# Reordering the loads ahead of the first expert layer: the second batch's rows before weight block 5, and the rows for the last transform in column halves

## The chip, the cores and the metric

The kernel runs on one core of one Trainium2 chip. The metric is the device time of one execution in microseconds; the median of several runs is what is compared.

## The reference

Two stages, joined by a reshape. First a spectral mixing of each of 8 sequences of 3008 rows and 256 channels: a real Fourier transform along the rows, a product with a complex filter, and the inverse transform. Then a two-layer perceptron with the activation h / (1 + exp(-h)) on all 24064 rows.

```python
X = np.fft.rfft(x, axis=1)                      # x: (8, 3008, 256)
Y = X * (filt_r + 1j * filt_i)[None]
y = np.fft.irfft(Y, n=3008, axis=1)
t = y.reshape(24064, 256)
h = t @ w_in                                    # w_in: (256, 2048)
g = h * (1.0 / (1.0 + np.exp(-h)))
out = g @ w_out                                 # w_out: (2048, 256), float64 on entry like w_in
```

## The kernel before, in words

**The steady part.** The transforms are written as small matrix products (3008 = 47 x 64). The perceptron goes in 48 pairs of token groups by 8 steps; each step does a hidden part (`hidden`, matmuls of L756 into px and pyz) and a projection (`project`, L819 into acc), with a scheme that trades matmuls for sums. While one batch is in the perceptron, the transforms of the next one are worked in between the steps, at places listed by hand (`plan`, `put`). The order of the instructions on every engine is that of the program text.

**The opening.** Nothing can be hidden for the first batch (batch 0), so its transforms stand ahead of the first step. In order:

- Weight blocks 0 to 3 and the rows of batch 0 are loaded; small matmuls (`idle`) run meanwhile. Each weight block j is two loads of 256 KB, `raw`, one of w_in (L926) and one of w_out (L929). The weights come as 64-bit floats and are turned into 32-bit ones by hand: `bits` (DVE), `converted` (ACT), `rounded` and `placed` (DVE).
- ACT, SP and POOL load the filters and the tables (`load_filters`, d_t, e_t). SP then loads the table of the last transform into `wi_t` and weight blocks 4 to 7.
- `stage1_first`, `forward`, `multiply`, `add`, `inverse_first`: the first transform, the second, the filter and the inverse of the second, in 6 groups g. `rows_first` (L541, L543) copies each group's result out of PSUM into two tiles q and stores each to `d2` in DRAM, 256 KB a store: ten stores from ACT's queue, two from SP's.
- `second["load_two"]` loads the first two of batch 1's eight pieces (768 KB) into `x_all` on SP, and weight block 8 is queued behind it. `stage1_first` reads x_all before that, as part of batch 0's rows.
- The rows of d2 (48 of them, for two halves h) come back into `t4`, for groups 0 to 3 of `stage3`, the last transform. `load_t4_rows(k)` (L571) loads the 16 rows that groups 2k and 2k + 1 of the inverse have made: one load for each h, 16 packets of 16 KB. `SPREAD` says on which partitions the 16 rows stand, and the table in wi_t has its rows in the same places (`ws_tbl`). Six loads in all, on SP.
- While they come, DVE and ACT convert weight blocks 4 to 8, PE runs the first transform of batch 1's two pieces (`stage1`, L345), and then 16 filler products (`idle_wide`, L1055), which write a bank that nobody reads.
- `stage3(0)` to `stage3(3)` (L586) run on PE; `copy` (L600) evicts them to `y` on ACT and DVE. When PE has read wi_t for the last of them, SP reloads it in the plain order (L1173), then loads batch 1's third and fourth pieces and weight blocks 10 to 13.
- From y, `tokens` makes the sums ty, and the first step begins (px, L756).

The loads and stores of SP's and ACT's queues carry completion semaphores that are used again in turn.

Of the kernel before, what the change touches and what calls it, by code (L numbers as in the profile page):

```python
# [56 lines left out]
NS, NG = 24, 6  # L57
# [12 lines left out]

SPREAD = (32, 1), (1, 2), (0, 2)


ORDER = [i for g in range(NG) for i in (g, g + 6, 17 - g, 23 - g)]
# [94 lines left out]
def kernel(  # L171
# [9 lines left out]
    nc = tc.nc  # L181
    ctx.enter_context(tc.manual_schedule())

    wf_host, wx_host, wq_host, wi_host, d_host, e_host = dft_tables()
# [1 line left out]
    wx_dram = nc.inline_tensor(wx_host, name="wx_tbl")  # L186
    wq_dram = nc.inline_tensor(wq_host, name="wq_tbl")
    wi_dram = nc.inline_tensor(wi_host, name="wi_tbl")
    ws_host = wi_host.copy()
    for k, (first, by) in enumerate(SPREAD):  # L190
        for h in range(2):
            ws_host[64 * h + first:64 * h + first + 15 * by + 1:by] = wi_host[64 * h + 16 * k:64 * h + 16 * k + 16]
    ws_dram = nc.inline_tensor(ws_host, name="ws_tbl")
    d_dram = nc.inline_tensor(d_host, name="d_tbl")
    e_dram = nc.inline_tensor(e_host, name="e_tbl")

# [26 lines left out]
    wi_t = cpool.tile([128, N1], FP32)  # L223
# [27 lines left out]
    def bank(b, name, spare=None):  # L251


        if early[0] is None and spare in ("x", "yz"):
            return xps.tile([128, 2, C], FP32, name=name, tag=spare)
        if early[0] is None and spare is not None:
            return accps.tile([128, 2, C], FP32, name=name, tag=f"a{spare}")
        if early[0] is None:
            return fps.tile([128, 2, C], FP32, name=name, tag="f")
        early[0] += 1  # L260
        k = early[0] % 8
        if k < 2:
            return fps.tile([128, 2, C], FP32, name=name, tag="f")
        if k > 5:
            return xps.tile([128, 2, C], FP32, name=name, tag="x" if k == 6 else "yz")
        return accps.tile([128, 2, C], FP32, name=name, tag=f"a{k - 2}")

    def spectral(b):
# [3 lines left out]
        d2 = dpool.tile([2 * NS, 32, 2, C] if b > 0 else [2 * NS, 2, 32, C], FP32, name=f"d2_{b}", tag="d2")  # L272
        xs, us, t2s, banks, prods, halves, t4s = {}, {}, {}, {}, {}, {}, {}
# [290 lines left out]
                rows = d2[:, h, 4 * g:4 * g + 4] if b == 0 else d2[:, 4 * g:4 * g + 4, h, :]  # L564
                nc.sync.dma_start(out=t4s[g][64 * h:64 * h + 2 * NS], in_=rows)

        def load_t4_rows(k, queue=None):

            first, by = SPREAD[k]
            for h in range(2):  # L570
                (queue or nc.sync).dma_start(out=us["t4"][64 * h + first:64 * h + first + 15 * by + 1:by],  # L571
                                  in_=d2[16 * k:16 * k + 16, h, 0:16])

        def stage3(g, home=None):

# [26 lines left out]
        def evict_y(g, h):  # L602
# [4 lines left out]

        return dict(us=us, store_rows=store_rows, evict_y=evict_y, evict_t1=evict_t1, halves=halves, load_first=load_first, stage1_first=stage1_first, fill_first=fill_first, load_x=load_x, load_two=load_two, sums=sums, stage1=stage1, reverse_x=reverse_x,
                    load_fold=load_fold, fold=fold, stage1_fold=stage1_fold, evict_fold=evict_fold,
                    load_t2=load_t2, forward=forward, multiply=multiply, add=add, inverse=inverse, inverse_first=inverse_first, rows_first=rows_first, even=even, rows=rows, load_t4=load_t4, load_t4_rows=load_t4_rows, stage3=stage3)  # L610

    pending = []

# [290 lines left out]
    def load_weights(j, queue=None):  # L904

        if j in (8, 11, 12, 13):
            pool, tag = (t4pool, "t4") if j in (11, 12) else (upool, "u")
            raw = pool.tile([128, 2, 512], U32, name=f"raw_{j}", tag=tag)
        else:

            if j in (0, 2):
                t = ypool.tile([128, 2, HALF], FP32, name=f"raw_{j}", tag="y")
                raws.setdefault("tiles", []).append(t)
                raws["at"] = t.rearrange("p a n -> p (a n)").bitcast(U32)[:, 0:2048]
                raws["y"] = raws["at"]
                raws.setdefault("first", raws["at"])
            elif j == 4:
                raws["at"] = spool.tile([128, 2048], U32, name=f"raw_{j}", tag="s")
            elif j == 6:
                raws["at"] = gpool.tile([128, 2048], U32, name=f"raw_{j}", tag="g")  # L920
            elif j in (9, 14):
                raws["at"] = raws["y"]
            at = 1024 * (j in (1, 3, 5, 7, 10, 15))
            raw = raws["at"][:, at:at + 1024].rearrange("p (w n) -> p w n", w=2)
        queue = queue or nc.sync
        queue.dma_start(  # L926
            out=raw[:, 0].rearrange("p (a n) -> p a n", a=2),
            in_=moe_w_in.bitcast(U32)[:, 256 * j:256 * j + 256].rearrange("(a p) n -> p a n", p=128))
        queue.dma_start(out=raw[:, 1], in_=moe_w_out.bitcast(U32)[128 * j:128 * j + 128, :])  # L929
        raws[j] = raw  # L930
# [78 lines left out]
    def weights(*js, queue=None):  # L1009
        for j in js:  # L1010
            if wide:
                load_weights(j, queue)
# [5 lines left out]
    def converted(*js):  # L1018
        if wide:
            convert_weights(*js)  # L1020
# [30 lines left out]
    def idle_wide(n, ps=None, rhs=None):  # L1051

        ps = ps or bank(0, "idle")
        for _ in range(n):
            nc.tensor.matmul(out=ps[:, 0], lhsT=wx_t, rhs=wide_rows if rhs is None else rhs,  # L1055
                             start=True, stop=True)

    wide_rows = d_t[0:96].rearrange("p s r n -> p (s r n)")[:, 0:256]
    idle(27)

    part, second = spectral(0), spectral(1)
    weights(0, 1, 2, 3)
    place = part["load_first"]()
# [10 lines left out]
    load_filters(queues, 4, 2 * NG)  # L1074
    nc.scalar.dma_start(out=d_t[:, 16:NS], in_=d_dram[:, 16:NS])
    nc.scalar.dma_start(out=e_t[:, 2:NG], in_=e_dram[:, 2:NG])
    nc.sync.dma_start(out=wi_t, in_=ws_dram.ap())
    weights(4, 5, 6, 7)

    signed = []  # L1080
    for i in range(2):
        t = typool.tile([128, 2, 2, 2, 128], FP32, name=f"signed_{i}", tag="ty")
# [26 lines left out]
    for k in range(16):  # L1109
        part["stage1_first"](k, 2)  # L1110
        if k in whole:
            part["stage1_first"](whole[k], 3)
    second["load_two"]()
    weights(8)
    part["forward"](0, fill=4)
    placed(0, 1)
    for g in range(1, 4):
# [31 lines left out]
    inverse(5)  # L1149
    bits(6, 7, 8)  # L1150
    for k in range(2):
        part["load_t4_rows"](k)
    part["load_t4_rows"](2)
    converted(4, 5)
    placed(2, 3)
    weights(9)
# [10 lines left out]
    gp.tensor_copy(out=gate, in_=w_t[:, 4, A11, 0, 0:1])  # L1167
    for u in range(2):
        second["store_rows"](u)
    idle_wide(16)  # L1170
    for g in range(4):
        part["stage3"](g)
    nc.sync.dma_start(out=wi_t, in_=wi_dram.ap())  # L1173
    second["load_x"](2)
    weights(10, 11, 12)
    second["load_x"](3)
# [7 lines left out]
    for b in range(1, B):  # L1184
        plan(b, second if b == 1 else spectral(b))
# [81 lines left out]
```

## Time and profile before

| | |
|---|---|
| median of 3 runs | 2579.2 us (2575.68 to 2580.06) |
| the profiled execution | 2579.25 us, of which its span is 2577.4 us |
| mean granted clock of TensorE | 0.995 |
| PE, DVE, ACT, POOL busy | 99%, 65%, 42%, 17% of the span |
| first stage 3 matmul that runs on, first px | 69.10 us, 76.94 us |

The profile is of one execution. Times in it are microseconds from the start of the span. PE is the matmul, PEld the load of its stationary operand, DVE, ACT, POOL and SP are the vector, scalar, GpSimd and sync engines; a q behind an engine's name is its sequencer, which issues DMAs. The matmuls of 32-bit floats stand in the profile as two records each. "x_all<-in_x_dram" is a transfer from the input x to the tile x_all.

### The profile page before, as it was taken

To read this page: it belongs to the slowest core of one execution; us is meant where nothing else is said; L and a number is where in the kernel's file an instruction comes from. 1 tells how busy PE (TensorE), PEld (TensorE's weight loads), DVE (VectorE), ACT (ScalarE), POOL (GpSimd) and SP (SyncE) were. 2 spreads that over 40 slices of the span, in tenths; PEclk is the share of its full clock that TensorE was granted. 3 is DMA by queue.
4 is the path that set the end of the run, shared out by engine and by line. 5 is a ranking of instruction groups with operands and counts; after the bars stand their busy time and mean duration, and the time that the engine had idled before them with its cause. 6 is when DMAs were issued, how large, how long until landed. Compare 5 with 4: busy or idle time off the path is not lost.

```text
span 2577.4 us, 47850 instructions
## 1 busy us (share of the span) xinstructions
PE 2553.1 (99%) x18714; PEld 2196.6 (85%) x18714; DVE 1664.4 (65%) x3589; ACT 1090.4 (42%) x3019; POOL 430.3 (17%) x688
## 2 busy tenths in 40 slices
PE   8999999999999999999999999999999999999998
PEld 6688888888888888888888888888888888888987
DVE  7766666676666666666666676666666666555554
ACT  3544444444444444444444444444444444444443
POOL 4212111111122111311121111211121112101101
PEclk9899999999999999999999999999999999999999
DMA  9522232222223222322233122331232211200011
GB/s 291 158 60 52 70 79 63 60 68 72 59 64 69 70 65 55 79 71 67 59 70 80 49 66 59 79 80 46 66 86 64 68 41 34 59 18 16 9 17 16
DMA packets 198554, 171.06 MB, mean 66 GB/s; under 512 B 122068, under 2 KB 173380, under 8 KB 197348
## 3 DMA queue, kind: packets, MB, share of 16 engines
q1 hardware_dynamic: 176056, 117.06, 19.9%
q0 software_dynamic: 17344, 45.70, 5.6%
q10 hardware_dynamic: 4928, 5.24, 0.7%
q8 instruction: 147, 2.41, 0.4%
q14 instruction: 79, 0.65, 0.1%
HBM read 96.07 MB, written 81.26 MB: 69 GB/s over the span
## 4 chain that ended last, share of the span: by engine, by line
PE 96%; DMA 2%; DVE 0%; ACT 0%; issue 0%; SPq 0%; ACTq 0%; DVEq 0%
PE acc L819 44%; PE px L756 26%; PE pyz L756 19%; PE pd L586 3%; PE pb L467 2%; PE pc L510 2%; PE pf L434 1%; DMA filt<-in_filt_i_dram 0%; PE pa L354 0%; DMA w_t<-in_x_dram 0%; DMA d_t<-d_tbl 0%; PE pa L345 0%; DMA x_all<-in_x_dram 0%; DMA d<-q 0%; DMA w_t<-d 0%; DMA t<-d 0%
## 5 line engine op out<-in xcount | busy, mean ns | idle before, releaser
L819 PE MATMUL acc<-g,w_t 128*128 128x256 f32 (+1 forms) x5376 | 1509.2, 375 | 0.4 <-DVE g L727 0.4
L819 PEld LDWEIGHTS acc<-g,w_t 128*128 128x128 f32 x5376 | 1021.6, 190 | 115.7 <-DVE g L727 0.8
L727 DVE TENSOR_TENSOR g<-pyz,abc 128x256 f32<-128x256 f32 (+1 forms) x1152 | 480.0, 417 | 621.6 <-ACT abc L777 356.2
L727 DVE TENSOR_TENSOR g<-g 128x256 f32<-128x256 f32 (+3 forms) x1152 | 599.4, 520 | 196.7 <-ACT g L760 183.5
L756 PE MATMUL px<-ty,w_t 128*128 128x256 f32 (+1 forms) x2304 | 679.4, 377 | 1.1 <-ACT abc L771 0.6
L760 ACT ACTIVATE g<-g 128x256 f32<-128x256 f32 (+1 forms) x1152 | 472.9, 410 | 250.2 <-DVE g L727 250.2
L727 POOL TENSOR_TENSOR s<-s 128x256 f32<-128x256 f32 (+1 forms) x329 | 255.0, 792 | 1417.5 <-DVE s L839 1321.0
L756 PEld LDWEIGHTS px<-ty,w_t 128*128 128x128 f32 x2304 | 432.7, 190 | 65.5 <-issue 6.2
L756 PE MATMUL pyz<-y,w_t 128*128 128x256 f32 (+1 forms) x1536 | 454.0, 377 | 0.0
L756 PEld LDWEIGHTS pyz<-y,w_t 128*128 128x128 f32 x1536 | 283.9, 190 | 47.6 <-DVE g L727 6.8
L771 ACT COPY abc<-px 128x256 f32<-128x256 f32 (+1 forms) x384 | 141.3, 368 | 372.9 <-PE px L756 372.9
L777 ACT COPY abc<-px 128x256 f32<-128x256 f32 (+1 forms) x384 | 141.5, 369 | 339.0 <-PE px L756 338.1
L760 ACT ACTIVATE g<-px 128x256 f32<-128x256 f32 (+1 forms) x384 | 145.8, 380 | 300.9 <-PE px L756 300.8
L756 PE MATMUL px<-y,w_t 128*128 128x256 f32 (+1 forms) x768 | 232.7, 385 | 0.8 <-DVE y L600 0.8
L756 PE MATMUL pyz<-ty,w_t 128*128 128x256 f32 (+1 forms) x768 | 225.8, 376 | 0.3 <-DVE g L727 0.2
L756 PEld LDWEIGHTS px<-y,w_t 128*128 128x128 f32 x768 | 140.4, 190 | 33.0 <-DVE y L606 5.3
L756 PEld LDWEIGHTS pyz<-ty,w_t 128*128 128x128 f32 x768 | 144.5, 190 | 19.2 <-DVE g L727 1.5
L764 ACT COPY abc<-px 128x256 f32<-128x256 f32 (+1 forms) x384 | 135.4, 353 | 52.7 <-PE px L756 52.7
L586 PEld LDWEIGHTS pd<-wi_t,t 48*64 48x64 f32 x3840 | 61.1, 135 | 25.1 <-ACT g L760 16.4
L446 POOL DMA_DIRECT2D d<-tf x144 | 71.6, 504 | 29.2 <-DVE tf L442 29.2
L839 ACT COPY s<-acc 128x512 f32<-128x512 f32 (+1 forms) x94 | 54.2, 577 | 47.6 <-PE acc L819 47.4
L869 DVE STREAM_TRANSPOSE o<-s 128x256 f32<-128x256 f32 x192 | 73.9, 423 | 0.4 <-issue 0.3
(136 smaller groups left out, 1269.9 us busy)
## 6 DMA issues: line engine op xcount, KB each, us to landing
t<-d SPq DMA_DIRECT2D x120, 192.0 KB
t<-d SPq DMA_DIRECT2D x84, 256.0 KB
d<-q POOLq DMA_DIRECT2D x84, 256.0 KB, 2.7
out_dram<-o SPq DMA_DIRECT2D x636, 32.0 KB
d<-tf POOLq DMA_DIRECT2D x144, 96.0 KB, 3.2
xr<-in_x_dram SPq DMA_DIRECT2D x6, 1472.0 KB
x_all<-in_x_dram SPq DMA_DIRECT2D x72, 96.0 KB
x_all<-xr SPq DMA_DIRECT2D x72, 96.0 KB
```

The source lines that it names most:

```text
L446: nc.gpsimd.dma_start(out=d1[k // 2, :, k % 2, n0:n0 + 4], in_=us["tf"][32 * k:32 * k + NS].rearrange("p q n c -> p (q n) c"))
L467: nc.tensor.matmul(out=ps[k][32 * j:32 * j + 32, ri, :], lhsT=d_t[rows, 4 * g + at, ri, :], rhs=rhs, start=True, stop=True)
L586: nc.tensor.matmul(out=ps[h][c0:c0 + 64, cb, i, :], lhsT=t4[rows, i, 128 * cb + c0:128 * cb + c0 + 64], rhs=wi_t[rows, :], start=True, sto ...
L727: eng.tensor_tensor(out=out, in0=in0, in1=in1, op=op)
L756: nc.tensor.matmul(out=out, lhsT=w_t[:, jp, c, 0], rhs=rhs, start=start, stop=True, skip_group_check=True)
L760: nc.scalar.activation(out=g[:, k, 0:n], in_=g[:, k, 0:n] if src is None else src, func=AFT.Silu)
L764: nc.scalar.copy(out=sums[:, 0, 0:n], in_=xo)
L771: nc.scalar.copy(out=sums[:, 1, 0:n], in_=xo)
L777: nc.scalar.copy(out=sums[:, 2, 0:n], in_=xo)
L819: nc.tensor.matmul(out=acc[pair][i][:, h, 0:n], lhsT=w_t[:, jp, c, 1], rhs=g[:, k, 0:n], start=(jp == 0 and h == 0), stop=last, skip_group ...
L839: copy(out=s[:, 2 * i:2 * i + 2, 0:n], in_=acc[pair][i][:, :, 0:n])
L869: v.transpose(out=o[:, :, h, :], in_=results[pair][:, ((2, 6), (4, 1))[chunk][h], :])
```

## The change

The rows of all groups stay where d2 has them: partitions 64h to 64h + 47. `load_t4_columns(k)` replaces `load_t4_rows(k)`: for each h one load of all 48 rows, but of 8 of the 16 columns, 48 packets of 8 KB. There are four loads in place of six. Columns 0 to 7 serve groups 0 and 1 of stage 3, columns 8 to 15 groups 2 and 3. The table wi_t is loaded once, in its plain order; ws_tbl and the reload are gone. Weight blocks 4 to 7 are issued later in the program, and `load_two` stands between block 4 and block 5; block 8 follows block 7. The filler has 12 products in place of 16.

```diff
-SPREAD = (32, 1), (1, 2), (0, 2)
...
-    ws_host = wi_host.copy()
-    for k, (first, by) in enumerate(SPREAD):
-        for h in range(2):
-            ws_host[64 * h + first:64 * h + first + 15 * by + 1:by] = wi_host[64 * h + 16 * k:64 * h + 16 * k + 16]
-    ws_dram = nc.inline_tensor(ws_host, name="ws_tbl")
...
-        def load_t4_rows(k, queue=None):
-
-            first, by = SPREAD[k]
+        def load_t4_columns(k):
+
             for h in range(2):
-                (queue or nc.sync).dma_start(out=us["t4"][64 * h + first:64 * h + first + 15 * by + 1:by],
-                                  in_=d2[16 * k:16 * k + 16, h, 0:16])
+                nc.sync.dma_start(out=us["t4"][64 * h:64 * h + 2 * NS, 8 * k:8 * k + 8],
+                                  in_=d2[:, h, 8 * k:8 * k + 8])
...
-    nc.sync.dma_start(out=wi_t, in_=ws_dram.ap())
-    weights(4, 5, 6, 7)
-
+    nc.sync.dma_start(out=wi_t, in_=wi_dram.ap())
     signed = []
...
             part["stage1_first"](whole[k], 3)
+    weights(4)
     second["load_two"]()
-    weights(8)
+    weights(5, 6, 7, 8)
     part["forward"](0, fill=4)
...
     for k in range(2):
-        part["load_t4_rows"](k)
-    part["load_t4_rows"](2)
+        part["load_t4_columns"](k)
     converted(4, 5)
...
         second["store_rows"](u)
-    idle_wide(16)
+    idle_wide(12)
     for g in range(4):
         part["stage3"](g)
-    nc.sync.dma_start(out=wi_t, in_=wi_dram.ap())
     second["load_x"](2)
```

More of the change, by code (lines that the diff above doesn't have):

```diff
@@ L609, in spectral @@
                     load_fold=load_fold, fold=fold, stage1_fold=stage1_fold, evict_fold=evict_fold,
-                    load_t2=load_t2, forward=forward, multiply=multiply, add=add, inverse=inverse, inverse_first=inverse_first, rows_first=rows_first, even=even, rows=rows, load_t4=load_t4, load_t4_rows=load_t4_rows, stage3=stage3)
+                    load_t2=load_t2, forward=forward, multiply=multiply, add=add, inverse=inverse, inverse_first=inverse_first, rows_first=rows_first, even=even, rows=rows, load_t4=load_t4, load_t4_columns=load_t4_columns, stage3=stage3)
     pending = []
```

## The prediction

> **What bounds the kernel now.** I read the page first, then the busy time by stretches.
>
> ```profile
> span 2577.4 us, 47850 instructions
> PE 2553.1 (99%) x18714; PEld 2196.6 (85%) x18714; DVE 1664.4 (65%) x3589; ACT 1090.4 (42%) x3019; POOL 430.3 (17%) x688
> ```
>
> PE is busy for 99% of the span. The stretches (columns: length, then PE, PEld, DVE, ACT and POOL busy, granted clock, DMA share, GB/s) show where it is not, and at what clock:
>
> ```profile
> 57.00:64.10 7.10, 7.08 (x33) 5.89 (x31) 7.07 (x18) 7.04 (x13) 0.00 (x0) 1.00 1.08 288
> 64.10:66.00 1.90, 0.00 (x0) 0.00 (x0) 1.87 (x6) 1.90 (x5) 0.00 (x0) 1.00 1.08 259
> 66.00:67.80 1.80, 0.00 (x0) 0.00 (x0) 1.80 (x4) 1.77 (x4) 0.00 (x0) 0.52 0.80 159
> 69.10:76.20 7.10, 7.07 (x254) 6.91 (x254) 2.95 (x7) 2.17 (x5) 4.18 (x9) 0.50 0.32 82
> 77.00:86.50 9.50, 8.40 (x18) 5.22 (x19) 7.38 (x18) 4.01 (x10) 0.00 (x0) 0.50 1.01 286
> 88.00:2550.00 2462.00, 2461.46 (x17867) 2122.52 (x17866) 1588.70 (x3431) 1046.66 (x2929) 398.64 (x621) 1.00 0.24 60
> ```
>
> From 88 us to 2550 us PE idles 0.5 us. A change of the opening is therefore worth what it moves the first px matmul (76.94 us), plus what it alters of the half clock between 66 and 86.5 us. Next, the chain of waits in the opening:
>
> ```profile
> 43.29 8.54 DMA x_all<-in_x_dram
> 51.91 0.37 ACTq L543
> 53.95 3.01 DMA d<-q
> 57.66 4.00 DMA d<-q
> 61.74 0.48 SPq L571
> 62.27 6.70 DMA w_t<-d
> 69.10 7.12 PE pd L586 x254
> 76.94 1.19 PE px L756 x2
> ```
>
> Read upwards: px waits for stage 3 (pd, L586), stage 3 for the sixth and last t4 load (L571), the last pair of t4 loads for the last store of block 0's rows (d<-q), and ACT's sixth store, at 51.91, for x_all. That store does not read x_all, so the wait is for the load's completion semaphore, which the store is to use again: x_all is the eighth DMA before it on the two queues (x_all, two of weight block 8, five stores). PE's own timeline shows the hole:
>
> ```profile
> 57.01 7.07 PE L1055 MATMUL idle<-d_t,wx_t 96*128 96x256 f32 x32
> 67.84 0.42 PE L586 MATMUL pd<-wi_t,w_t 48*64 48x47 f32 x2 [3.76 <-DMA w_t<-d]
> 156.26 1.15 PE L586 MATMUL pd<-wi_t,t 48*64 48x47 f32 x64
> ```
>
> The 32 records of the filler (two per call, 0.221 us each) end at 64.08, and PE stands 3.76 us for t4. Stage 3 costs 7.12 us at half clock; later, at full clock, 64 records took 1.15, so 256 would take at most 4.6.
>
> **The change, part by part.**
>
> *x_all ahead of block 5.* SP's order after block 4 becomes x_all, blocks 5 to 8. SP issued block 5's first load at 38.49; x_all takes that place. Its other wait is for stage 1, whose last read of x_all on PE ended before 30 us, so it holds nothing behind it. The same 768 KB now pass ahead of blocks 5 to 7: 786 kB at 347 GB/s (the rate in 38.5 to 45 us) are 2.3 us, at 229 GB/s (45 to 50.7 us) 3.4 us. By the count of eight, ACT's first store will wait for block 5's first load. In the kernel before that load was down by 45.32 at the latest, when the first store left, so the store leaves between 45.3 and 48.7; I take 47.2. Behind it in ACT's queue stand the other copies L541, and PE's third inverse waits for the second of them. So ACT and PE slip by about 1.9 us there. On the other side the wait at 51.91 goes, which cost 1.5 us (the copy was done at 50.43). Ten ACT stores at 1.03 us from 47.2 put the last at 56.5 instead of 56.11: 0.4 us, covered, because the stores land at the pace of the transfers (376 GB/s in 51 to 57 us), and the last of all is SP's at 57.66, which DVE sets. I keep 61.74 for the first moment when all rows are stored. Block 5 is first read by DVE at 50.4 and blocks 6 to 8 at 57.5, when they are down in either order: nothing. If that cover were gone, each microsecond would be paid in full.
>
> *Blocks 4 to 7 issued later in the program, one wi table.* SP has no other instruction between the old and the new place: nothing. The reload of wi_t (L1173) waited 12.2 us for stage 3 and held x_all's third piece and blocks 10 to 13 behind it on SP; these now go out from 65 us on. Nobody waited for them (x_all's third piece is read at 89.2), so no gain. They are queued behind the t4 loads and can delay only POOL's eight d<-t stores (issued 72.2 to 76.3, first read by loads at 135.7): nothing.
>
> *Six row loads become four column halves.* The bytes are the same, 1536 KB. Before, four of six loads needed only earlier rows and were issued from 58.21 on, under the last stores. Now each needs all 48 rows, so none can leave before 61.74. In exchange groups 0 and 1 of stage 3 need the first pair alone. Rows for the rate:
>
> ```profile
> 62.50:66.50 4.00, 1.58 (x8) 1.05 (x6) 3.93 (x10) 3.97 (x9) 0.00 (x0) 0.95 0.94 222
> 162.20:164.20 2.00, 2.00 (x11) 1.76 (x10) 0.93 (x3) 0.77 (x3) 0.00 (x0) 1.00 0.95 219
> 169.20:171.90 2.70, 2.70 (x14) 2.31 (x14) 1.18 (x3) 1.06 (x3) 0.00 (x0) 1.00 0.53 147
> 8.50:15.00 6.50, 5.46 (x44) 5.27 (x43) 5.66 (x12) 5.04 (x9) 0.00 (x0) 1.00 1.00 423
> ```
>
> The first holds the old t4 loads, the second and third later t4 loads of the same 48 rows (4 KB each; the third with gaps), the fourth the 128-row load of x, the fastest here. I take 222 GB/s, the same data at the same place: 1.573 MB are 7.1 us, a pair 3.5. To this come the lags before and behind the data: the page gives 2.7 us from issue to landing for POOL's 256 KB stores, 0.7 of which are data at 376 GB/s, so 2.0 (an estimate). The first pair is there at 61.74 + 2.0 + 3.5 = 67.2, the second at 70.8.
>
> Stage 3 at half clock: groups 0 and 1 from 67.2 to 70.8, groups 2 and 3 from 70.8 to 74.4, against 76.2: **-1.8 us**. DVE is free from 71.5 and takes the last y copy as before. At 423 GB/s the pair is there at 65.6 and the end is 72.7 (-3.5); at 147 the second pair is there at 74.4 and the end 78.0 (+1.8).
>
> The Trainium skill ("DMA: Bandwidth & Descriptors", Specifications) gives a core about 358 GB/s from HBM. By that the four loads take 4.4 us and stage 3 ends near 73.0, a gain of 3.2; the old t4 loads ran at 222, and the row decides.
>
> *Filler 16 to 12.* 4 x 2 x 0.221 = 1.8 us less on PE. Ended at 64.08, it would end at 62.3; with PE's slip of 0 to 3.4 in the inverses it ends at 62.3 to 65.7, by my values 64.2. The hole before stage 3 is then 1.5 to 4.9 us, by my values 3.0, against 3.76. The clock fell at 66 us, about 2 us into the old hole, so I expect the half clock again and cost this edit at nothing.
>
> The skill speaks against this edit ("TensorE: Matmul & The Clock Gate", HAM oscillation): PE holes over some 3.4 us bring the half clock. By it a hole of 4.9 is cold and one of 3.0 may stay warm; the trace shows the fall within 2 us, with no hole between 2 and 3.76 us to tell.
>
> **Sum.** The profiled execution took 2579.25 us (span 2577.4, 1.9 around it), the median is 2579.2. So 2579.25 - 1.8 = 2577.4.
>
> **The rivals.**
>
> A, the sum above: 2577.4, own range 2575.7 to 2581.0 (the two rates).
>
> B, the clock stays full. If PE slips by 2 to 3 us the hole is under 2.5 us and the clock may never fall. Groups 2 and 3 then take 2.3 us from 70.8, so stage 3 ends at 73.1 (-3.1). In the 77 to 86.5 stretch PE was busy 8.40 at half clock; at full clock up to 4.2 go, and ACT's and DVE's links in that first step give back part: I take 2.8, between 1.5 and 4.2. Together -5.9: 2573.3, range 2572 to 2574.6. For it: the shorter hole. Against: stage 3's own small matmuls ran 7 us without raising the clock, so they may not hold it either.
>
> C, slower: the first-store wait takes the place of the one removed. x_all spent 8.54 us from issue to landing. If it costs block 5 as much, ACT's first store leaves at up to 53.9 and the last (nine steps of 1.03) at 63.1, 7.0 late; less the 1.8 won that is 2584.4, and 2586.2 if the column halves win nothing. It decides from a hold of 3.3 us on (1.5 of the wait removed plus 1.8). For it: ACT stands in order, and PE's inverses behind it. Against: at 53.9 the data path would have run dry, and the rates give 2.3 to 3.4.
>
> D, nothing: the columns lose by starting late what the halves win, 2579.2.
>
> **How the numbers follow.** A 0.42, B 0.40, C 0.13, D 0.05. About 0.2% (5.2 us) is what a measurement of this kernel can tell from no change. Faster by more: B but for 0.02 at its slow end, 0.38. Slower by more: 0.12, C but for its mild end. Within: the other 0.50. The range 2571.0 to 2583.0 covers A and D, all of B with a microsecond to spare, and the mild end of C; it leaves out most of C.
>
> **What would show it.** ACT's sixth store no longer waits for x_all; the first leaves near 47. The t4 loads are four, issued 61.7 to 63.4; the first pd after 67, a second wait near 70.8, the last pd near 74.4, first px near 75. Clock 0.5 in that stretch for A, 1.0 for B. I am wrong if the first store leaves after 49, if the stores end after 62.5, if the four loads take over 9 us, or if anything changes after 88 us.

## Result, and the profile after

| | before | after |
|---|---|---|
| median, 20 runs each on one chip | 2577.55 us (2573.26 to 2580.06) | 2581.63 us (2578.54 to 2584.5) |
| the profiled execution (its span) | 2579.25 us (2577.4) | 2583.78 us (2582.0) |
| first px matmul | 76.94 us | 81.07 us |

The change makes the kernel slower by 4.1 us: the ratio is 1.0016, interval [1.001, 1.0022]. In the two profiles the first px is 4.13 us later, and the execution 4.53 us longer.

Line numbers of the kernel after are 7 lower: pd is L579, px L749, the filler L1048. The page's totals, and then the busy time by stretches (length, PE, PEld, DVE, ACT, POOL busy, granted clock, DMA share, GB/s):

```profile
span 2582.0 us, 47829 instructions
PE 2553.3 (99%) x18706; PEld 2196.5 (85%) x18706; DVE 1664.5 (64%) x3589; ACT 1091.4 (42%) x3019; POOL 430.4 (17%) x688
```

```profile
61.70:67.00 5.30, 5.30 (x26) 4.40 (x24) 5.23 (x14) 5.24 (x10) 0.00 (x0) 1.00 0.85 164
72.94:76.55 3.61, 3.61 (x122) 3.46 (x122) 0.87 (x2) 0.47 (x1) 2.79 (x7) 0.50 1.06 310
76.55:79.84 3.29, 0.01 (x1) 0.00 (x0) 0.00 (x0) 0.00 (x0) 1.48 (x4) 0.50 1.08 380
81.07:90.60 9.53, 8.43 (x18) 5.24 (x19) 7.40 (x18) 4.02 (x10) 0.00 (x0) 0.50 0.43 156
92.20:2554.20 2462.00, 2460.44 (x17865) 2122.25 (x17864) 1587.55 (x3430) 1047.69 (x2928) 398.76 (x621) 1.00 0.24 59
```

PE's busy time is unchanged (2553.3 against 2553.1). The new row is the third: for 3.29 us PE, DVE and ACT all stand, with four records of stage 3 still to do, while the DMA engines are full (1.08). The last row is 1 us less busy than in the kernel before (2460.44 against 2461.46): something is lost after the opening too. PE's timeline and the chain of waits:

```profile
47.75 6.81 PE L521 MATMUL pc<-w_t,signed 64*128 64x256 f32 x31 [3.38 <-ACT q L535]
61.70 5.34 PE L1048 MATMUL idle<-d_t,wx_t 96*128 96x256 f32 x24
66.97 0.31 PE L579 MATMUL pd<-wi_t,w_t 48*64 48x47 f32 x2
68.65 2.56 PE L579 MATMUL pd<-wi_t,w_t 48*64 48x47 f32 x128 [1.36 <-DMA w_t<-d]
72.94 3.62 PE L579 MATMUL pd<-wi_t,w_t 48*64 48x47 f32 x122 [1.73 <-DMA w_t<-d]
79.84 0.45 PE L579 MATMUL pd<-wi_t,w_t 48*64 48x47 f32 x4 [3.29 <-issue]
81.07 1.19 PE L749 MATMUL px<-y,w_t 128*128 128x256 f32 x2 [0.77 <-DVE y L593]
```

```profile
37.69 10.26 DMA raw<-in_moe_w_in_dram
48.02 0.38 ACTq L537
61.88 0.22 SPq L564
63.41 9.39 DMA w_t<-d
76.56 3.29 issue
```

ACT's first store waits for block 5's first load and leaves at 48.02. The first t4 load leaves at 61.77, as before's all-stored time of 61.74. Both column pairs come later than forecast, and then comes a wait that nothing in the forecast had: "issue", a hole that no semaphore explains.

**What the hole is.** PE's own instructions are fetched by DMA too: among the queues of the 16 DMA engines the profile's page lists 147 packets of 16 KB on an "instruction" queue, q8. 147 x 256 = 37632, about PE's 2 x 18706 matmul records and weight loads: a packet is 256 instructions, 128 records with their loads. The DMA view, after in the first fence and before in the second, each time the stretch ahead of the packet and, behind the dots, the packet itself:

```profile
DMA packets 1520, 3.38 MB, mean 221 GB/s; under 512 B 159, under 2 KB 927, under 8 KB 1328
q1 hardware_dynamic: 1520, 3.38, 99.1%
...
q8 instruction: 1, 0.02, 36.5%
```

```profile
DMA packets 553, 1.52 MB, mean 149 GB/s; under 512 B 108, under 2 KB 364, under 8 KB 492
q1 hardware_dynamic: 553, 1.52, 65.9%
...
q8 instruction: 1, 0.02, 32.8%
```

In after the stretch 62 to 77.3 us holds no packet of q8; it comes in 77.3 to 77.5 (start 77.33), and PE goes on at 79.84. In before the stretch 62 to 72.2 holds none and it comes at 72.26. And ahead of it the DMA engines of the kernel before stood empty (windows of before):

```profile
70.00:72.20 2.20, 2.20 (x93) 2.20 (x91) 1.50 (x4) 0.85 (x2) 0.19 (x1) 0.50 0.00 0
72.20:76.20 4.00, 3.98 (x149) 3.81 (x142) 0.55 (x1) 1.32 (x3) 4.00 (x8) 0.50 0.52 132
```

They were empty because batch 1's third piece (into x_all) and blocks 10 to 13 stood on SP behind the reload of wi_t, which waited for stage 3 and left at 76.24. In after these loads leave from 64.87 us on.

### The profile page after: what moved, and what is told of

Same layout as the page of the kernel before. It is cut to its first block, busy times and chain, and to the rows that moved or that the text cites. A ratio compares the mean times of both kernels' runs of the same rounds, so it can differ in the third digit from the quotient of the medians.

```text
span 2582.0 us, 47829 instructions
## 1 busy us (share of the span) xinstructions
PE 2553.3 (99%) x18706; PEld 2196.5 (85%) x18706; DVE 1664.5 (64%) x3589; ACT 1091.4 (42%) x3019; POOL 430.4 (17%) x688
## 4 chain that ended last, share of the span: by engine, by line
PE 96%; DMA 2%; DVE 0%; issue 0%; ACT 0%; SPq 0%; ACTq 0%; DVEq 0%
PE acc L812 44%; PE px L749 26%; PE pyz L749 19%; PE pd L579 3%; PE pb L461 2%; PE pc L504 2%; PE pf L428 1%; DMA raw<-in_moe_w_in_dram 1%; PE pa L339 0%; PE pa L348 0%; DMA w_t<-in_x_dram 0%; DMA filt<-in_filt_r_dram 0%; DMA w_t<-d 0%; PE pc L521 0%; DMA d_t<-d_tbl 0%
## 5 line engine op out<-in xcount | busy, mean ns | idle before, releaser
L749 PE MATMUL px<-ty,w_t 128*128 128x256 f32 (+1 forms) x2304 | 679.4, 377 | 1.1 <-ACT abc L764 0.6
L749 PEld LDWEIGHTS px<-ty,w_t 128*128 128x128 f32 x2304 | 432.5, 190 | 65.4 <-issue 6.2
L749 PE MATMUL pyz<-y,w_t 128*128 128x256 f32 (+1 forms) x1536 | 454.0, 377 | 0.0
L749 PEld LDWEIGHTS pyz<-y,w_t 128*128 128x128 f32 x1536 | 284.1, 190 | 47.3 <-DVE g L720 6.9
L749 PE MATMUL px<-y,w_t 128*128 128x256 f32 (+1 forms) x768 | 232.7, 385 | 0.8 <-DVE y L593 0.8
L749 PE MATMUL pyz<-ty,w_t 128*128 128x256 f32 (+1 forms) x768 | 225.8, 376 | 0.2 <-DVE g L720 0.2
L749 PEld LDWEIGHTS px<-y,w_t 128*128 128x128 f32 x768 | 140.4, 190 | 33.0 <-DVE y L599 5.8
L749 PEld LDWEIGHTS pyz<-ty,w_t 128*128 128x128 f32 x768 | 144.6, 190 | 18.8 <-DVE g L720 1.2
L579 PEld LDWEIGHTS pd<-wi_t,t 48*64 48x64 f32 x3840 | 61.5, 135 | 26.4 <-ACT g L753 16.4
```

What stands on the lines that cost most here:

```text
L579: nc.tensor.matmul(out=ps[h][c0:c0 + 64, cb, i, :], lhsT=t4[rows, i, 128 * cb + c0:128 * cb + c0 + 64], rhs=wi_t[rows, :], start=True, sto ...
L749: nc.tensor.matmul(out=out, lhsT=w_t[:, jp, c, 0], rhs=rhs, start=start, stop=True, skip_group_check=True)
```

## The experiments

All were timed against the kernel before on the same chip, 11 runs each. An interval reaches some 2.3 us to each side, so a single difference of 1 or 2 us is not established; what carries the reading is that the differences repeat in pairs and that the profiles show the place. The ratio is estimated from all runs and is not the quotient of the two medians, so the two columns can differ: run 17's 0.9993 stands for 1.8 us where its medians differ by 3.1, run 2's 1.0005 for 1.3 where they differ by 1.8. "Lag" is worked out from the trace: from PE's crossing of the packet end before (128 records earlier) to the start of the packet.

| kernel | difference of medians, us | ratio [interval] | all rows stored to px, us | lag of packet, us | hole at packet end, us |
|---|---|---|---|---|---|
| before | 0 | 1 | 15.2 | 0.1 | none |
| after, first chip | +4.08 | 1.0016 [1.001, 1.0022] | 19.3 | 6.7 | 3.29 |
| 1 after, reload kept | +2.10 | 1.0007 [0.9998, 1.0016] | 16.3 | 3.9 | 1.16 |
| 2 before, no reload | +1.76 | 1.0005 [0.9996, 1.0014] | 16.8 | 3.2 | 1.97 |
| 3 before, x_all first | +0.42 | 1.0005 [0.9996, 1.0014] | 15.9 | 0.3 | none |
| 4 after, six wide fillers | +3.91 | 1.0012 [1.0003, 1.0021] | 19.3 | 5.3 | 3.40 |
| 5 before, columns only | +0.43 | 1.0001 [0.9992, 1.001] | 15.9 | 1.8 | none |
| 6 run 1, block 9 held too | +5.23 | 1.0018 [1.0009, 1.0026] | 16.2 | 3.6 | none |
| 7 before, two queues | -0.25 | 0.9998 [0.9989, 1.0007] | 13.4 | 0.3 | none |
| 8 run 7, x_all first | +0.53 | 1.0005 [0.9996, 1.0014] | 11.0 | 0.7 | 1.19 |
| 9 run 5, filler 12 | +1.18 | 1.0004 [0.9995, 1.0013] | 15.8 | 1.9 | none |
| 10 run 1, filler 16 | +0.96 | 1.0005 [0.9995, 1.0014] | 16.0 | 3.3 | none |
| 11 before, filler 24 | -0.02 | 1.0 [0.9991, 1.0009] | 14.9 | 0.2 | none |
| 12 run 7, filler 24 | -0.73 | 0.9995 [0.9986, 1.0004] | 12.4 | 0.6 | none |
| 13 run 5, no reload | +2.25 | 1.0008 [0.9999, 1.0017] | 18.5 | 4.5 | 2.10 |
| 14 after again | +4.83 | 1.0017 [1.0008, 1.0026] | 17.9 | 4.1 | 2.19 |
| 15 run 7, filler 27 | +0.53 | 1.0002 [0.9993, 1.0011] | 12.5 | 1.1 | 1.25 |
| 16 before, filler 16 x 384 | -1.50 | 0.9994 [0.9985, 1.0003] | 14.9 | 0.3 | none |
| 17 run 7, filler 16 x 384 | -3.10 | 0.9993 [0.9984, 1.0002] | 14.8 | 0.2 | none |
| 18 after, filler 16 x 192 | +2.26 | 1.0009 [1.0, 1.0018] | 18.1 | 4.5 | 1.59 |

"All rows stored to px" runs from the first t4 load that waits for all stores (with columns the first, with rows the last pair) to the first px; in runs 7, 8, 12, 15 and 17 it is the last load on SP alone and is not to be set against the others.

**The reload of wi_t as a gate: runs 1, 2 and 6.** Run 1 keeps the now useless reload in the kernel after; run 2 takes it from the kernel before by giving the two layouts a tile each; run 6 is run 1 with block 9's loads behind the reload too.

```diff
     for g in range(4):
         part["stage3"](g)
+    nc.sync.dma_start(out=wi_t, in_=wi_dram.ap())
     second["load_x"](2)
```

> The changed kernel, but with the reload of wi_t kept behind stage 3 on SP (it loads the same table again). It holds batch 1's third piece and weight blocks 10 to 13 back until PE has read wi_t for the last time, as in the kernel before. Theory F (PE ran out of instructions in stage 3: the 3.3 us hole before its last 4 records ends after a 16 KB packet of the instruction queue, which had to go through DMA rings full of the early x and weight loads): the hole is gone, first px near 77.4 instead of 81.07, time 3.3 to 3.7 us under the changed kernel, near that of before (within 1 us). Rival K (the four column loads are the loss: later and slower, and the hole is a wait that the profile does not show on the same loads): the hole stays, time as the changed kernel, 4 us over before.

```diff
-    nc.sync.dma_start(out=wi_t, in_=ws_dram.ap())
+    nc.sync.dma_start(out=ws_t, in_=ws_dram.ap())
+    nc.sync.dma_start(out=wi_t, in_=wi_dram.ap())
...
-                                rhs=wi_t[rows, :], start=True, stop=True)
+                                rhs=(ws_t if b == 0 and g < 4 else wi_t)[rows, :], start=True, stop=True)
...
-    nc.sync.dma_start(out=wi_t, in_=wi_dram.ap())
     second["load_x"](2)
```

> The kernel before with a second tile for the table: the spread table is loaded into its own tile, the plain one into wi_t at the start, and the reload behind stage 3 is gone. Rows, filler and the place of x_all are those of before. Theory F: the loads of x and of weight blocks 10 to 13 leave from about 64 us, the instruction packet that went at 72.26 us goes late, and PE stands 2 to 4 us near the end of stage 3: 2 to 4 us slower than before, px near 79 to 81. Rival K: no change (within 1 us).

```diff
     converted(4, 5)
     placed(2, 3)
-    weights(9)
...
     nc.sync.dma_start(out=wi_t, in_=wi_dram.ap())
+    weights(9)
     second["load_x"](2)
```

> The changed kernel with the reload of wi_t kept and weight block 9 moved behind it, so that nothing is queued behind the four column loads until stage 3 is done. Theory F (the instruction packet, asked for near 70.5 us, waits behind whatever is in the rings): the packet goes by 73, the hole before the last 4 records, 3.29 us in the changed kernel and 1.16 with the reload alone, is gone; px 1 us earlier than with the reload alone; time 0.5 to 1.5 us under that kernel, 2 to 3 us under the changed one. Rival T (the packet is asked for only when PE starts the second half, near 73, and then takes its usual time): packet near 74.5 and hole near 1.2, as with the reload alone.

Putting a transfer of 24 KB that nobody needs into the kernel after wins back 2.0 us (+4.08 to +2.10), less than the 3.3 to 3.7 expected, and a hole of 1.16 us stays; taking the needed one out of the kernel before loses 1.8 (2 to 4 expected) and makes the hole (PE's timeline of run 2):

```profile
69.06 6.09 PE L587 MATMUL pd<-ws_t,w_t 48*64 48x47 f32 x242 [0.83 <-DMA w_t<-d]
77.12 0.67 PE L587 MATMUL pd<-ws_t,w_t 48*64 48x47 f32 x12 [1.97 <-issue]
```

Run 6 shows no hole in stage 3, yet was the slowest of all by its median; in its profile block 9 was then late itself (DVE's timeline):

```profile
83.90 0.43 DVE L944 TENSOR_SCALAR e<-raw 128x512 uint32<-128x512 uint32 x1 [2.68 <-DMA raw<-in_moe_w_out_dram]
```

So the gate must hold what nobody waits for, and only that. Nor did the hole go for the reason expected. The packet came at 75.01 and not by 73: it followed PE's start of the second half, as the rival T had it, with the DMA engines all but empty ahead of it (PE's timeline, and a row of windows):

```profile
74.08 3.79 PE L579 MATMUL pd<-wi_t,w_t 48*64 48x47 f32 x126 [1.71 <-DMA w_t<-d]
```

```profile
73.20:75.00 1.80, 0.92 (x36) 0.95 (x37) 0.76 (x2) 0.00 (x0) 0.53 (x2) 0.50 0.01 5
```

The hole of 1.2 us that T expected did not come, since this half ran at half clock: PE reached the packet's end at 77.4, 2.4 us behind the packet's start.

**Where the hole stands: run 4.** The filler as 6 products over 512 columns: the same time, 12 records fewer.

```diff
-            nc.tensor.matmul(out=ps[:, 0], lhsT=wx_t, rhs=wide_rows if rhs is None else rhs,
+            nc.tensor.matmul(out=ps.rearrange("p a c -> p (a c)"), lhsT=wx_t, rhs=wider_rows,
...
-    idle_wide(12)
+    idle_wide(6)
```

> The changed kernel with its filler as 6 products of 512 columns in place of 12 of 256: PE's time is the same, but 24 instruction records fewer stand ahead of stage 3 (each product is two matmuls with a weight load each). Theory F: the place where PE runs out of instructions moves by 24 records, that is out of stage 3 and four products into the first step, which PE reaches near 81, after the packet: the hole before the last 4 records is gone, px near 77.4, time 3 to 3.7 us under the changed kernel. Rival K: the hole stays where it is in the work, time as the changed kernel.

The hole did not go, it moved:

```profile
69.13 2.54 PE L579 MATMUL pd<-wi_t,w_t 48*64 48x47 f32 x128 [1.33 <-DMA w_t<-d]
73.46 0.46 PE L579 MATMUL pd<-wi_t,w_t 48*64 48x47 f32 x6 [1.79 <-DMA w_t<-d]
77.32 3.45 PE L579 MATMUL pd<-wi_t,w_t 48*64 48x47 f32 x120 [3.40 <-issue]
```

It now stands after 2 + 128 + 6 = 136 records of stage 3 in place of 252. 12 records fewer ahead put the next packet end 12 records later, at 264, and so the one before it at 136: the count fits to the record. It fits in all nine profiles with such a hole: 4 records from the end with 24 filler records, 12 with 32, 34 with 54, 120 with 12. In all nine PE went on 2.3 to 2.8 us after the packet's start. A hole stands where the packet starts later than about 2.5 us ahead of PE's arrival.

The table's lag, taken with the DMA share between the crossing and the packet, says what makes it late. With row loads and the reload it is 0.1 to 0.7 us (1.1 in run 15); in runs 8 and 15, where stage 3 ran at full clock, that was enough for a hole. With row loads and the freed loads (run 2) it is 3.2 us, at a DMA share of 1.10. With columns PE itself has to wait for t4's second pair 6 or 14 records behind the crossing (but for run 4, where the ends lie elsewhere), and the packet starts only behind that wait: 0.3 to 1.5 us behind its end with the reload (runs 1, 5, 6, 9, 10), 2.3 to 4.4 us without it (after, runs 13, 14, 18), at a DMA share of 1.05 to 1.07. In run 1, as in run 6, the engines were nearly empty for 1.1 us ahead of the packet at 74.55:

```profile
73.40:74.50 1.10, 1.10 (x84) 1.10 (x77) 0.19 (x2) 0.23 (x1) 0.60 (x2) 0.89 0.04 13
```

So the freed loads make the packet late, and the column halves do it as well, by PE's own wait; why the packet waits for PE there is not shown.

**The place of x_all: runs 3, 7 and 8.**

```diff
-    weights(4, 5, 6, 7)
-
...
+    weights(4)
     second["load_two"]()
-    weights(8)
+    weights(5, 6, 7, 8)
```

> The kernel before with one edit of the change alone: weight blocks 4 to 7 issued later in the program and x_all ahead of block 5. Theory F with the clock: ACT's first store is held to about 48, PE stands 3.4 us before its third inverse, as in the changed kernel; PE's filler of 16 then ends near 69, when the rows are there, so no hole and a full clock in stage 3; the stores still land by 61.7. Stage 3 ends near 73.5 to 74, px near 74.5, time 2 to 6 us under before. Rival H (the hold of ACT's stores is the loss): px after 78, time 1 to 4 us over before.

```diff
-                (queue or nc.sync).dma_start(out=us["t4"][64 * h + first:64 * h + first + 15 * by + 1:by],
+                (nc.gpsimd if h else nc.sync).dma_start(out=us["t4"][64 * h + first:64 * h + first + 15 * by + 1:by],
```

> The kernel before with the three row loads of the half h = 1 issued from POOL's queue in place of SP's, so that loads of both halves run side by side. Theory P (the loads of one half run at 180 to 220 GB/s because the 48 rows of a half lie on one side of the partitions, where the 128-row load of x ran at 423): the six loads take some 2 us less, the last is there near 66.5 to 67.5 instead of 69.0, px 1.5 to 2.5 us earlier, time 1 to 4 us under before. Rival D (the reads from d2 in DRAM limit them): the same rate, px and time within 0.7 us of before.

> The kernel before with both: x_all ahead of block 5, and the row loads of h = 1 from POOL's queue. Rows, table, reload and filler of 16 are those of before. Theory P with F: the sum of the two, that is 1 to 4 us under before; in executions where x_all's place delays PE's inverses, the filler ends only when the rows are there. Rival D: within 1 us of before.

With x_all first, ACT's first store left 0.53 to 0.58 us after x_all had landed in all nine profiles of such kernels, when block 5's first load behind it was down too: the wait is real. It left on average at 47.3, against 45.0 with x_all behind (eleven profiles). But the mean of the time at which all rows were stored is the same, 61.5 us, in both (columns with x_all first: seven profiles; behind: three). Run 3 cost 0.4 us, within its interval; neither of its two expectations came. Run 7 left the time as it was (rival D), though px came 1.6 us earlier in its profile. Run 8 kept the full clock through stage 3, with a hole of 1.19 us in it, and gained nothing. By medians the place of x_all costs 0.42 (run 3), 0.92 (run 1 less 9), 0.53 (run 10 less 5) and 0.01 us (run 18 less 13, which differ in the filler's width too); whether that is more than nothing stays open.

**Columns and the filler's length: runs 5, 9 and 10,** a square of two edits around run 1.

```diff
-    part["load_t4_rows"](2)
+        part["load_t4_columns"](k)
...
-    nc.sync.dma_start(out=wi_t, in_=ws_dram.ap())
+    nc.sync.dma_start(out=wi_t, in_=wi_dram.ap())
```

> The kernel before with the four column loads and the plain table in place of the six row loads; the order of x_all and the weight blocks, the reload that holds the later loads, and the filler of 16 are those of before. Theory F with slow columns (a pair of column loads takes 4.3 us, none leaves before 61.7, and the late loads with block 9 behind them also hold up PE's instruction packet a little): first pair near 68.5, second near 72.8, px near 78, time 1 to 2.5 us over before. Rival X (the columns cost nothing; what was left over before with the reload kept is due to x_all's place): within 0.7 us of before.

```diff
-    idle_wide(16)
+    idle_wide(12)
```

> The kernel before with the column halves and the plain wi table (its reload kept), x_all's load where it was, and the filler of 12 calls in place of 16. It is the kernel of the run that kept the reload (2580.1) but for x_all's place, and the kernel of the run with columns alone (2578.1) but for the filler. Theory: of the 2 us between those two, x_all's place is the cause (ACT's stores held, a 2.6 us hole in PE's inverses): then this run is at 2578 to 2578.5, its first px matmul at 76 to 77 us. Rival: the shorter filler is the cause, since PE then stands for 3 to 5 us ahead of stage 3 and the clock falls for the whole stage: then it is at 2579.5 to 2580.5, px at 77.5 to 78.5.

```diff
-    idle_wide(12)
+    idle_wide(16)
```

> The kernel after with the reload of wi kept and the filler of 16 calls in place of 12: x_all is first, the columns are in. If x_all's place is the cause of the 2 us, this run is at 2579.5 to 2580.5 like the run with 12. If the shorter filler is the cause, it is at 2578 to 2578.5. The filler should end near 68.6 us in place of 67.0, close to where the first pair of columns lands (68.9), so the clock may stay full through stage 3; by the run with 12, where only the end of the stage was at half clock, that is worth 0.5 us at most, unless the first px step comes under full clock too (another 1 to 3).

The columns with everything else as before cost 0.43 us: about nothing, as rival X had it, and no gain. Filler 12 against 16 is +0.75 with x_all behind (1.18 - 0.43) and +1.14 with it first (2.10 - 0.96). Neither rival of run 9's expectation was right alone.

**The parts without the reload: runs 13 and 14.** Run 13 is run 5 without the reload, run 14 the kernel after unchanged.

```diff
     for g in range(4):
         part["stage3"](g)
-    nc.sync.dma_start(out=wi_t, in_=wi_dram.ap())
     second["load_x"](2)
```

> The kernel before with the column halves and the plain wi table loaded once: no reload, so x_all's third piece and blocks 10 to 13 leave from 65 us on. x_all's place and the filler of 16 calls are as before. It is the run with columns alone (2578.1) less the reload. Theory: the reload held those loads off the rings until stage 3 was done; without it PE's packet of instructions comes late and a hole of 2 to 3.5 us stands near the end of stage 3. Then this run is 1.5 to 2.5 us above the run with columns alone, 2579.6 to 2580.6, px at 78.3 to 79.5. Rival: the packet is late only together with x_all's earlier place or the shorter filler: then there is no hole, px is at 76 to 77 and the run is at 2578 to 2578.5.

> The kernel after once more, beside the run without the reload alone. If the four parts add up (columns 0 to 0.5, x_all's place 0.8, the filler 0.8, the reload 2), it is 3.5 to 4.1 us above the kernel before and 1 to 2 us above the other run, with the hole again 4 records before the end of stage 3. If the reload were all of it, the two runs would be equal.

Run 13 less run 5 is again 1.8 us for the reload alone (2.25 - 0.43), with a hole of 2.10 us; the theory held, the rival fell. Run 14 lies 2.6 above run 13, more than expected. Its own profiled execution was one of its fastest: all rows were stored at 58.60 us in place of 61.77, as x_all had landed at 44.70 in place of 47.46. So the opening as a whole varies by 3 us and more from one execution to the next, and single profiles are compared here within themselves only, by the last three columns of the table.

**The half clock and the packets: runs 11, 12 and 15 to 18.** Runs 11, 12 and 15 lengthen the filler by more calls (24, 24 and 27 in place of 16), so that it reaches to t4's landing.

```diff
-    idle_wide(16)
+    idle_wide(24)
```

> The kernel before with the filler of 24 calls in place of 16: 16 records of 0.221 us more, so that it ends near 67.6 us in place of 64.08, where the first t4 pair lands at 67.8; the hole of 3.76 us goes and the clock should stay full in stage 3. Theory that the half clock costs the time: stage 3 takes 3.6 us in place of 7.1, the end of the stage is at 72.7 to 73.5 and the kernel is at 2573 to 2575. Rival, the instructions: PE then reaches the next block of 256 instruction records 28 records before the end of stage 3, at about 72.3, and waits for it for 1 to 3 us; then px is at 75 to 76 and the kernel at 2576 to 2577. Rival, the first px step is bound by ACT and DVE and gives the gain back: no difference.

> The kernel before with the loads of the second half rows issued on POOL's queue and the filler of 24 calls. In the run with 16 calls the first matmul of stage 3 was at 66.43 and the stage ran at half clock from 67.52 to 74.6 (2577.4 us). With 24 the filler ends near 66.8 and the clock should stay full: stage 3 ends near 71.2, the first px matmul is near 72 to 73, and the kernel at 2573 to 2575. If the instruction packets bound it, a hole of 1 to 3 us comes ahead of the last 28 records and the kernel is at 2575.5 to 2576.5.

> The kernel before with the loads of the second half rows issued on POOL's queue and the filler of 27 calls: it ends near 67 us, where the first rows land. With 24 calls the profile had two holes of 1.5 and 0.7 us ahead of stage 3 and half clock in 69.3 to 72.7; px came 2.8 us earlier than before and the kernel was 0.7 us faster, within its interval. If those holes bring the half clock, it is gone here: stage 3 takes 3.7 us in place of 5.5, px is at 73 to 73.5, and the kernel is 1.5 to 3 us faster than before. If the clock falls all the same, it is at the time of the run with 24, 0 to 1 us faster.

All three won in the opening: counted from the end, the same PE record as before's at 90 us came 2.57, 3.67 and 2.43 us earlier. In the times nothing is left that stands out of the intervals. The trace shows two new holes in all three, where no kernel with 16 calls or fewer has one, and a third at 671 us in run 15: 1.3 to 1.4 us in sum (PE's timeline of run 11):

```profile
1293.42 2.06 PE L586 MATMUL pd<-wi_t,t 48*64 48x47 f32 x122
1296.17 0.32 PE L586 MATMUL pd<-wi_t,t 48*64 48x47 f32 x6 [0.69 <-issue]
1920.92 0.47 PE L756 MATMUL px<-y,w_t 128*128 128x240 f32 x1
1922.07 0.36 PE L756 MATMUL px<-y,w_t 128*128 128x240 f32 x1 [0.68 <-issue]
```

All five profiles of kernels with 12 calls have one at about 2235 to 2240 us (0.71 to 1.09 us), and no other has; first after, then before at the same place:

```profile
2236.16 2.06 PE L579 MATMUL pd<-wi_t,t 48*64 48x47 f32 x123 [0.26 <-DVE g L720]
2239.31 0.31 PE L579 MATMUL pd<-wi_t,t 48*64 48x47 f32 x3 [1.09 <-issue]
```

```profile
2232.68 2.07 PE L586 MATMUL pd<-wi_t,t 48*64 48x47 f32 x126 [0.26 <-DVE g L727]
2234.69 0.67 PE L756 MATMUL px<-y,w_t 128*128 128x240 f32 x2
```

Stage 3's small matmuls use up a packet's 128 records in 2.1 us, less than the 2.5 that PE took after the packet's start in the holes. Where a packet ends late in such a group, PE can run dry. A filler with other counts shifts every packet end behind it. Runs 16 to 18 change the filler's length and keep its 16 calls, by the width of a product (runs 16 and 17: before and run 7 with 384 columns; run 18: after with 192).

```diff
-            nc.tensor.matmul(out=ps[:, 0], lhsT=wx_t, rhs=wide_rows if rhs is None else rhs,
+            nc.tensor.matmul(out=ps.rearrange("p a c -> p (a c)")[:, 0:384], lhsT=wx_t, rhs=filler_rows if rhs is None else rhs,
...
+    filler_rows = d_t[0:96].rearrange("p s r n -> p (s r n)")[:, 0:384]
```

> The kernel before with a filler of the same 16 calls (32 matmul records), each over 384 columns in place of 256: it lasts 10.6 us in place of 7.1 and ends near 67 us, but PE's instructions keep their places. With 24 calls of 256 columns the start was won by 2.5 us at 90 us in the profile, and new PE holes of 0.7 to 1.0 us stood at 1296 and 1922 us, which no kernel with 16 calls has; the time was that of before. Theory that the 16 added records moved the ends of PE's instruction packets into places where PE is faster than the packets: no hole there now, and the kernel is 1.5 to 3 us faster than before, 2574.5 to 2576. Rival, those holes are chance: the time is again that of before, within 0.6 us.

> The same filler (16 calls over 384 columns) with the loads of the second half rows issued on POOL's queue. With 24 calls of 256 columns: 3.7 us won at 90 us in the profile, the two holes later, 2577.4 us in the end. Without the holes 2574 to 2575.5 is expected, 2 to 3.5 us below before; by chance alone 2577.4 again.

> The kernel after with a filler of 16 calls over 192 columns in place of 12 over 256: the same 5.3 us of filler, but PE's instructions again in the places that they have in the kernel before. All five profiles of kernels with 12 calls have a PE hole of 0.9 to 1.1 us at about 2236 us, none of those with 16 has it. If the shorter filler's loss is those moved packets, the hole is gone and the kernel is 0.8 to 1.5 us faster than after, about 2580.5 to 2581.3, 3 us above before. In stage 3 the packet then ends 12 records before the end in place of 4; the hole there stays. If the filler's loss lies in its length, the kernel is at 2582 like after.

No hole stands at 1296, 1922 or 2236 us in any of the three, as the packet theory had it. The times fit it or come close. Run 18, after's filler with its count taken back, came to 2580.47 us (expected 2580.5 to 2581.3), 1.8 us better than after on the first chip and 2.6 better than run 14, each against before beside it. Run 17 came to 2575.11 (expected 2574 to 2575.5). Run 16 lies 1.50 below before, the near edge of the 1.5 to 3 expected, and at 2576.71 it is above the 2574.5 to 2576. PE's timeline of run 18:

```profile
2234.22 2.08 PE L579 MATMUL pd<-wi_t,t 48*64 48x47 f32 x126 [0.26 <-DVE g L720]
2236.23 0.67 PE L749 MATMUL px<-y,w_t 128*128 128x240 f32 x2
```

Run 17 has the lowest median of all, 2575.11 us, 3.1 below before beside it, but its interval [0.9984, 1.0002] still holds 1: the likeliest version to beat both kernels, not one that is shown to. Its profiled execution (2579.71) was the longest of its 11 and ran stage 3 at half clock throughout, and run 16's first px came at 76.58, 0.4 us ahead of before's: where the gain of these two medians comes from is not shown.

## Why the prediction was wrong

**The step that failed: "Nobody waited for them (x_all's third piece is read at 89.2), so no gain."** The loads let loose by the dropped reload were priced by who reads them, and by POOL's stores behind them, "nothing". They had a third neighbour, PE's instruction packets. The packet came at 77.33 in place of 72.26, 4.4 us behind the start of stage 3's second half where it came 0.3 to 1.5 us behind it in the column kernels with the reload; PE stood 3.29 us, and the medians give 1.8 (run 2), 1.8 (run 13 less 5), 1.3 (run 18 less 10, which differ in the filler's width too) and 2.0 us (after less run 1). The profile of before raises the question by one row: DMA share 0.00 in 70 to 72.2 us, a quiet that the reload made.

**"I expect the half clock again and cost this edit at nothing": wrong, by another way than either of the two weighed.** The clock did fall, at 70.19 us. But the 8 records fewer move the packet ends, and a hole of 1.09 us comes at 2239 us, which run 18 takes away. By medians the edit costs 0.75, 1.14 and 1.8 us (after less run 18). "If anything changes after 88 us" was among the signs of being wrong, and it came.

**"Groups 0 and 1 from 67.2 to 70.8, groups 2 and 3 from 70.8": a term mis-sized.** Stage 3's two halves began at 68.65 and 72.94; 786 kB in those 4.29 us are 183 GB/s in place of 222. The freed loads are not the cause: with the reload (run 5) the halves were 4.40 us apart, and in run 6, where no other load was queued, 4.48 us, with the DMA engines full at 170 GB/s (its windows):

```profile
64.50:69.50 5.00, 3.50 (x18) 2.72 (x16) 4.93 (x11) 4.93 (x10) 0.00 (x0) 1.00 1.04 170
```

In the stretch with 222 the old loads came in packets of 16 KB, in the trace of run 6 the column halves come in packets of 8 KB; that the size makes the difference is not shown. Without the hole the stage would end near 76.7 (122 records are done at 76.55, four more take 0.03 us each), against 76.18 before and 74.4 forecast: 2.3 us of the forecast's error. Run 5 shows the same by the time, +0.43 in place of -1.8.

**What held.** ACT's first store was to leave at 47.2: 48.02 here, 47.3 in the mean of such kernels. All rows were to be stored at 61.74 as before: 61.77. The half clock, and its 9.5 us of the first step, came as in rival A. Rival C put the loss into ACT's wait; it was there, and PE's hole of 3.38 us too, but the transfers' pace covered it.

**The sum by the runs.** Means of the pairs: reload 1.7, filler 1.2, x_all's place 0.5, columns 0.4 (run 5 alone): 3.8, against 4.1 measured. No pair is clear of the intervals by itself. The first term is carried by four pairs that agree (1.3 to 2.0) and by the hole in every profile without the reload; the second by the hole near 2236 us in all five profiles with 12 calls and by run 18; the last two are too small to be told from nothing.

**The rule that bore on it.** The Trainium skill ("Runtime: NRT & Kernel Launch", Instruction fetch mechanics) describes blocks of 256 instructions, 16 KiB each, fetched over a queue of their own, and calls the price of crossing a block's end mostly hidden. The size agrees with the trace to the record. The price was hidden here too at nearly all of the 147 packets, but not where it bore on the change: PE stood 0.3 to 3.4 us where the DMA engines were full, where PE had itself been waiting, or where the instructions were short, and the measurement decides.

## What to carry to other kernels

A transfer that waits on an in-order queue also holds back what stands behind it, and that quiet may be worth more than the transfer costs: before removing a wait, look at the DMA share in the stretch where the freed loads will run, and count the instruction queues among those who need it. Where PE's code is a long straight line, a filler is better resized by the width of its products than by their number, since the number moves the end of every instruction packet behind it. And an "issue" hole on PE is a question for the instruction queue, not for semaphores, when a packet of that queue starts some 2.5 us ahead of the hole's end and the hole moves with the number of records ahead of it.

## What the hardware showed that was not expected

- In the nine holes of the opening PE went on 2.3 to 2.8 us after the start of a 16 KB instruction packet. The packet starts 0.1 to 0.3 us after PE crosses the packet end before it in before and runs 3, 7, 11, 16 and 17 (DMA share 0.00 to 0.43 ahead of it), 0.6 to 1.1 us after it in runs 8, 12 and 15 (0.00 to 0.08), and 3.2 to 6.7 us after it with the freed loads (1.00 to 1.10). That it is asked for at that crossing would fit these times, but run 6 speaks against it: there it started 3.6 us after the crossing, the last 1.8 of them with empty engines, behind PE's own wait. No record shows the asking.
- The granted clock falls after much less idling than the 3.4 us that the Trainium skill names ("TensorE: Matmul & The Clock Gate", HAM oscillation). In run 17 holes of 1.73 and 0.78 us around two records came at 68 to 70.8 us, and the clock was half from 70.36 on. But for those at the ends of each trace, all stretches at half clock are multiples of 3.41 us (3.41, 6.83, 10.24, 13.65, 17.07, 20.48), which agrees with the fixed window of 3413 ns that the page describes (What's actually happening).

```profile
57.51 10.48 PE L1055 MATMUL idle<-d_t,wx_t 96*128 96x384 f32 x32
69.73 0.28 PE L586 MATMUL pd<-wi_t,w_t 48*64 48x47 f32 x2 [1.73 <-DMA w_t<-d]
70.79 7.07 PE L586 MATMUL pd<-wi_t,w_t 48*64 48x47 f32 x254 [0.78 <-DMA w_t<-d]
```
